# Startup loads on ScalarE's queue, spaced first scores and a re-planned attention stage: a decay-attention kernel with two dense layers

## The chip, the cores and the metric

The kernel runs on one core of one Trainium2 chip. The metric is the device time of one execution in microseconds; the number that counts is the median of several runs. One more execution is recorded by the hardware profiler, and all rows below come from it. The engines are PE (TensorE matmul; PEld is its weight load), DVE (VectorE), ACT (ScalarE), POOL (GpSimd) and SP (SyncE, which mostly issues DMAs).

## What is computed

Three layers follow each other on 4 batches of 8 heads, 576 tokens, head size 64 (2304 tokens of 512 features):

```
scores = q @ k.T / sqrt(64)
cum    = cumsum(log(clip(f, 1e-4, 1)), axis=-1)
scores = where(causal, -1e9, scores + cum[..., :, None] - cum[..., None, :])
attn   = exp(scores - max);  attn = attn / (sum(attn) + 1e-9)
x      = (attn @ v), heads side by side          # 2304 x 512
h = x @ w_in;  g = s * relu(h)**2 + b;  x = g @ w_out             # 512 -> 2048 -> 512
h = x @ w_in;  g = max(h, 0) + alpha * min(h, 0);  out = g @ w_out  # 512 -> 2048 -> 512
```

q, k, v, x and the outputs are fp32; the weights of the two dense layers come in 64-bit words and are split by the kernel into a high and a low part, so that each dense product is three matmul passes (high with high, low with high, high with low).

## The kernel before, in words

**One static order.** The program does not write its instructions in order of the source. It lists tasks (engine, planned cost, what they read and write, a priority), and `Scheduler.run` plays them through in a simulated time and issues on each engine, when that engine is free in the plan, the ready task with the lowest priority. What comes out is a fixed instruction order for each engine; on the chip the engines then wait for each other by semaphores. The priorities come from the table `PLAN`. A list of two options (`pick(PLAN["nr"], ...)`) lets the plan take whichever engine is free; a one-letter entry fixes the engine.

**Unread products.** While the plan's time is below `FILL` (50 us) and PE has nothing ready in the plan, `filler()` (L388) issues a 128x256 bf16 matmul of a tile of ones into a spare PSUM tile `h`. Nobody reads it. These products are in the static order too: each costs its time whether PE would have waited there or not.

**Startup.** SP's queue loads, in this order, the q and k rows of units 0 and 1 (`lk`, L314), the forget factors `ft`, the selector matrix `sel`, the first part of the causal mask, then weights (`raw`), identity and v. DVE clamps `ft` (L492), ACT takes the logarithm (L493, after a table load L478), DVE scans it into `ct` (L494), DVE and POOL make scaled and split copies (L497 to L506) that go out to DRAM and come back as extra rows of later `lk` tiles.

**Attention.** Work is cut into units: units 0 to 3 are two heads each with the 128-row chunks 0 and 1, then single heads of batch 0 with the chunks 2, 3 and 4, then whole heads of batches 1 to 3. For a chunk: scores on PE (L675 in fp32; L670 and L671 in high and low parts from the 13th unit on; unit 0 alone is L678, L679 and L681, where PE itself adds the decay from `ct` and `sel`), masked maximum on DVE (L689), exponential on ACT (L694), reciprocal of the sum on DVE (L697, L698), the norm, that is the division by the sum (L705, always POOL here, `nr="p"`), transposes on PE (L745), their copies out of PSUM on ACT (L754, L756), products with v on PE (L798), and the split of the result into high (L804) and low (L809). POOL also makes the high part of k and q (L610, L613), their difference (L619, `kl="p"`), and the low part of weights (L439); ACT and DVE convert the weights (L422; L413, L416, L419; L429).

**Dense part.** Between the attention tasks the plan puts the first half of the first dense layer for the blocks of 256 tokens 0 to 5 (L847 products into `h`, L884 into `a`). From about 334 us on only dense work is left: 512-wide products on L847, L882 and L887, with ACT and DVE making `r` and `g` between them. The last 128 rows of the output leave through two copies of one accumulator into one tile `o` and one DMA.

The lines that matter below:

```python
    startup(("sp", 200, lambda: load(ft, f)), w=["f"])
    hi="a", ev="a", xh="va", gh="va", kl="p", nr="p", lo="p",
    if eng == "pe" and free["pe"] <= now + 1e-6 and now < FILL and self.filler is not None and self.filler():
```

## Time and profile before

| | |
|---|---|
| median of 3 runs | 1007.63 us (1007.58, 1007.63, 1012.58) |
| the profiled execution's own time | 1007.88 us |
| its span, first to last instruction | 1006.1 us |
| outside the span | 1.78 us |
| PE busy | 997.2 us, 99% of the span |
| PE's share of the chain that ended last | 96% |

PE is the engine that sets the time. "Busy" on PE is not the same as useful: it includes the unread products. From 333.8 us to 1002.2 us PE is busy without a gap.

### The profile page before, as it was taken

The numbers are of one execution on the slowest core, as the hardware profiler recorded it, in microseconds if no ns is written. First come the engines' busy times: TensorE is split into PE (matmuls) and PEld (weight loads), VectorE is DVE, ScalarE is ACT, GpSimd is POOL, SyncE is SP. The second block draws the span as 40 slices with busy tenths as digits, with TensorE's granted clock in tenths as the row PEclk, the third lists the DMA queues.
The fourth block names the chain that finished last, engine by engine and source line by source line (L and its number), as shares of the span: only waits on it lengthen the run. The fifth ranks groups of instructions, "written<-read, shape, count | busy, mean of one in ns | idle before, by whom it ended". The sixth has DMA issues, their size and how long they took to land.

```text
span 1006.1 us, 15607 instructions
## 1 busy us (share of the span) xinstructions
PE 997.2 (99%) x5705; PEld 835.2 (83%) x5705; DVE 555.8 (55%) x1262; ACT 450.6 (45%) x1067; POOL 236.4 (24%) x275
## 2 busy tenths in 40 slices
PE   9999999999999999999999999999999999999998
PEld 7678889997989889888888888888888888888897
DVE  5888876576575688988342789323222322322232
ACT  5777766557566445555232445222222222222232
POOL 4656765465364144211000121000000000000000
PEclk9999999999999999999999999999999999999999
DMA  7765436234431544447352665003002100200010
GB/s 215 242 191 163 146 107 213 83 104 125 141 116 31 190 144 127 135 136 263 96 171 70 218 225 174 1 1 125 1 1 84 42 1 1 83 1 1 1 42 22
DMA packets 45519, 106.45 MB, mean 106 GB/s; under 512 B 4492, under 2 KB 23524, under 8 KB 44516
## 3 DMA queue, kind: packets, MB, share of 16 engines
q1 hardware_dynamic: 45444, 105.46, 32.7%
q8 instruction: 45, 0.74, 0.3%
q14 instruction: 30, 0.25, 0.1%
HBM read 77.65 MB, written 24.26 MB: 101 GB/s over the span
## 4 chain that ended last, share of the span: by engine, by line
PE 96%; ACT 1%; DMA 1%; DVE 1%; issue 1%; POOL 0%; ACTq 0%; POOLq 0%; SPq 0%
PE h L847 24%; PE k L847 16%; PE b L882 11%; PE a L884 9%; PE b L887 9%; PE a L882 9%; PE t L798 5%; PE t L745 4%; PE s L670 2%; PE a L887 2%; PE s L671 2%; PE h L388 2%; PE s L675 1%; DMA raw<-in_wi_dram 1%; ACT e L694 0%
## 5 line engine op out<-in xcount | busy, mean ns | idle before, releaser
L847 PE MATMUL h<-x,i 128*128 128x256 f32 (+1 forms) x1344 | 256.4, 340 | 0.3 <-DVE r L858 0.3
L847 PEld LDWEIGHTS h<-x,i 128*128 128x128 f32 x1344 | 210.9, 189 | 31.5 <-DVE r L858 0.9
L847 PE MATMUL k<-x,i 128*128 128x512 f32 (+1 forms) x672 | 153.4, 377 | 0.0
L847 PEld LDWEIGHTS k<-x,i 128*128 128x128 f32 x672 | 120.7, 188 | 25.5
L882 PE MATMUL b<-o,g 128*128 128x512 f32 x480 | 121.1, 393 | 0.0
L875 DVE TENSOR_TENSOR g<-r,g 128x512 fp32r<-128x512 f32 (+1 forms) x80 | 51.1, 639 | 121.0 <-ACT g L864 121.0
L705 POOL TENSOR_SCALAR e<-e,rec 128x128 f32<-128x128 f32 (+4 forms) x144 | 89.6, 634 | 90.5 <-DVE rec L698 40.8
L882 PEld LDWEIGHTS b<-o,g 128*128 128x128 f32 x480 | 90.2, 188 | 20.5
L439 POOL TENSOR_TENSOR i<-cv,i 128x512 fp32r<-128x512 f32 x32 | 49.7, 1554 | 243.9 <-ACT i L429 243.8
L864 ACT CAST g<-r 128x512 fp32r<-128x512 f32 (+1 forms) x78 | 45.1, 578 | 137.5 <-PE b L882 87.6
L884 PE MATMUL a<-g,o 128*128 128x256 f32 x768 | 104.5, 285 | 0.0
L882 PE MATMUL a<-o,g 128*128 128x512 f32 x384 | 98.8, 393 | 0.0
L884 PEld LDWEIGHTS a<-g,o 128*128 128x128 f32 x768 | 96.8, 190 | 1.2 <-issue 0.7
L887 PE MATMUL b<-g,o 128*128 128x512 f32 x384 | 95.3, 394 | 0.0
L873 DVE SCALAR_TENSOR_TENSOR g<-r,small,g 128x256 fp32r<-128x256 f32 (+1 forms) x104 | 70.6, 679 | 41.2 <-ACT g L866 40.1
L694 ACT ACTIVATE e<-e,ngm 128x128 f32<-128x128 f32 (+4 forms) x144 | 84.2, 586 | 15.4 <-DVE ngm L689 13.4
L887 PEld LDWEIGHTS b<-g,o 128*128 128x128 f32 x384 | 72.0, 188 | 16.8
L882 PEld LDWEIGHTS a<-o,g 128*128 128x128 f32 x384 | 71.1, 188 | 15.1
L866 ACT ACTIVATE g<-r,small 128x256 fp32r<-128x256 f32 (+1 forms) x90 | 53.3, 592 | 61.3 <-PE b L887 31.3
L689 DVE CUSTOM_DVE_ANT_0 e<-s,mask 128x128 f32<-128x128 f32 (+4 forms) x144 | 66.9, 480 | 18.3 <-PE s L671 7.3
L745 PE MATMUL t<-ident,e 128*128 128x128 f32 (+1 forms) x400 | 64.9, 275 | 3.5 <-ACT pt L754 2.1
L860 DVE SCALAR_TENSOR_TENSOR r<-k,sg_t,r 128x512 f32<-128x512 f32 (+1 forms) x40 | 27.9, 697 | 73.2 <-ACT r L854 73.2
(102 smaller groups left out, 1252.0 us busy)
## 6 DMA issues: line engine op xcount, KB each, us to landing
raw<-in_wi_dram SPq DMA_DIRECT2D x32, 512.0 KB
raw<-in_wo_dram SPq DMA_DIRECT2D x32, 512.0 KB
x<-x_d SPq DMA_DIRECT2D x7, 2048.0 KB
rawqk<-in_qk_dram SPq DMA_DIRECT2D x24, 576.0 KB
x_d<-o SPq DMA_DIRECT2D x36, 256.0 KB
v<-in_v_dram SPq DMA_DIRECT2D x20, 320.0 KB
x_d<-x SPq DMA_DIRECT2D x6, 1024.0 KB
out_dram<-o SPq DMA_DIRECT2D x18, 256.0 KB
```

Of the source, the lines that this page charges most:

```text
L689: nc.vector.tensor_tensor_reduce(e.t[0:rows, k0:k1], st_.t[0:rows, 0:w], mask[0:rows, m0:m0 + w], -0.125 if u.f32 else -1.0, init, ALU.add ...
L694: nc.scalar.activation(x, x, AF.Exp, bias=ng[0:rows, col:col + 1], scale=-1.0, accum_out=sm[0:rows, col:col + 1])
L705: eng.tensor_scalar(x, x, rc[0:rows, col:col + 1], 1.0, ALU.mult, ALU.mult)
L745: nc.tensor.transpose(pp.t[0:kw, i * P:i * P + P], e.t[:, P * kb:P * kb + kw], ident)
L798: nc.tensor.matmul(o.t[64 * j:64 * j + 64, a - q0:z - q0], vb.t[0:kr, kb, j, :], uu.pt[jj].t[0:kr, kb * PTS + a:kb * PTS + z], start=(i == ...
L847: nc.tensor.matmul(ps.t[:, 0:w], wv[:, wl, kc, :], x.t[:, kc, xl, x0:x0 + w], start=(n == 0), stop=(n == 3 * KC - 1))
L866: eng.activation(g.t[:, 0, 0:w], r.t[:, 0:w], AF.Identity, bias=b_t)
L873: nc.vector.scalar_tensor_tensor(g.t[:, 1, 0:w], r.t[:, 0:w], b_t, h, ALU.add, ALU.subtract)
L875: nc.vector.tensor_tensor(g.t[:, 1, 0:w], r.t[:, 0:w], h, ALU.subtract)
L882: nc.tensor.matmul(acc[u].t, g.t[:, gl, u * P:u * P + P], wo.t[:, wl, :], start=(first and i == 0), stop=end)
L884: nc.tensor.matmul(acc[u // 2].t[:, T * (u % 2):T * (u % 2) + T], wo.t[:, wl, u * P:u * P + P], g.t[:, gl, 0:w], start=(first and i == 0 a ...
L887: nc.tensor.matmul(acc[u].t[:, 0:w], wo.t[:, wl, u * P:u * P + P], g.t[:, gl, 0:w], start=(first and i == 0), stop=end)
```

## The change

Five things are changed at once.

1. `ft`, `sel` and the first part of the mask are issued by ScalarE's queue (a planner engine "aq"), ahead of ScalarE's first table load, and no longer by SP.
2. An unread product is put ahead of each of the three parts of unit 0's scores: 12 in all.
3. Loads are shorter: unit 0's `lk` comes in two halves of one head each; single-head units of batch 0 load their q and k only from the first row of q that they use.
4. The planner's cost for chunk 4 is changed, and the table `PLAN` is new. Norms may go to POOL, ACT or DVE (`nr="pav"`), the difference of k to POOL or DVE (`kl="pv"`), the high part of weights to DVE or ACT.
5. The last 128 output rows leave as two halves with a tile and a DMA of their own: columns 0 to 255 by DVE and SP's queue, 256 to 511 by ACT and ACT's queue.

```diff
-    hi="a", ev="a", xh="va", gh="va", kl="p", nr="p", lo="p",
+    hi="va", ev="a", xh="va", gh="av", kl="pv", nr="pav", lo="p",
...
-    startup(("sp", 200, lambda: load(ft, f)), w=["f"])
+    st.append(task(("aq", 200, lambda: nc.scalar.dma_start(ft, f)), w=["f"], prio=-300.0))
...
-    startup(("sp", 200, lambda: load(sel, sel_in)), w=["sel"])
+    st.append(task(("aq", 100, lambda: nc.scalar.dma_start(sel, sel_in)), w=["sel"], prio=-250.0))
...
+                q0 = P * u.chunks[0]
+                load(u.lk.t.bitcast(F32)[0:64].rearrange("d a s -> d (a s)")[:, q0:2 * S],
+                     qk[n, 0:64].rearrange("d a s -> d (a s)")[:, q0:2 * S])
...
+        if u.pe_rows:
+            for j in range(2):
+                h = slice(QA * j, QA * j + QA)
+                task(("sp", 0.9 * kb_of(P * 4 * w), lambda h=h: load(u.lk.t.bitcast(F32)[0:64, :, h], qka[n // 2][:, :, h])), w=[(U, "raw", j)],
+                     bufs=[u.lk], prio=-200.0 if j == 0 else pr)
...
                         n = uu.heads[j]
+                        sc.filler()
                         nc.tensor.matmul(x, lk[0:64, 0, q], lk[0:64, 1, k], start=True, stop=False)
+                        sc.filler()
                         nc.tensor.matmul(x, ct[:, 128 * c:128 * c + rows], sel[:, 0, n:n + 1].to_broadcast([NHEAD, nn]),
                                          start=False, stop=False)
+                        sc.filler()
                         nc.tensor.matmul(x, sel[:, 1, n:n + 1].to_broadcast([NHEAD, rows]), ct[:, k0:k1], start=False, stop=True)
...
-                for h, (e, cols) in enumerate((("act", slice(0, 288)), ("dve", slice(288, DM)))):
+                for h, (e, cols) in enumerate((("dve", slice(0, 256)), ("act", slice(256, DM)))):
+                    if h:
+                        o = R["o"].buf()
...
-                task(("sp", kb_of(P * 2048), lambda row=row, o=o: load(out[row:row + P, :], o.t)), r=[("ot", row, 0), ("ot", row, 1)], w=[("out", row)],
-                     bufs=[o], prio=epr)
+                    task((("sp", "act")[h], (kb_of(P * 1024), 600)[h],
+                          lambda f=(nc.sync.dma_start, nc.scalar.dma_start)[h], cols=cols, row=row, o=o: f(out[row:row + P, cols], o.t[:, cols])),
+                         r=[("ot", row, h)], w=[("out", row, h)], bufs=[o], prio=epr)
...
-        task(("sp", kb_of(P * 4 * (z - a)), lambda a=a, z=z: load(mask[:, a:z], mask_in[:, a:z])), w=[("mask", i)],
-             prio=PLAN["mp"] + PLAN["mq"] * (i > 0))
+        task(("sp" if i else "aq", kb_of(P * 4 * (z - a)), lambda i=i, a=a, z=z: (nc.sync if i else nc.scalar).dma_start(mask[:, a:z], mask_in[:, a:z])),
+             w=[("mask", i)], prio=PLAN["mp"] + PLAN["mq"] if i else -200.0)
```

**What the new order is at three places.** Line numbers of the changed kernel are higher by 8 to 27.

ScalarE at the start of the program, before:

```order
L478 ACT_TABLE_LOAD
L478 ACTIVATE small<-small 128x1
L493 ACTIVATE ft<-ft 32x256
L493 ACTIVATE ft<-ft 32x320
L503 ACT_TABLE_LOAD
```

and changed:

```order
L484 DMA ft<-in_f_dram 32x576
L487 DMA sel<-in_sel_dram 32x64
L1021 DMA mask<-in_mask_dram 128x256
L486 ACT_TABLE_LOAD
L486 ACTIVATE small<-small 128x1
L501 ACTIVATE ft<-ft 32x256
L501 ACTIVATE ft<-ft 32x320
```

Three DMA issues now stand ahead of the table load on ACT; on SP they are gone from behind the loads of `lk`.

PE around the first scores (`s`, unit 0), with `h` the tile of the unread products, before:

```order
L388 MATMUL h_114<-unit 128x256
L678 MATMUL s_192<-lk_112 128x128
L679 MATMUL s_192<-sel,ct 128x128
L681 MATMUL s_192<-ct,sel 128x128
L678 MATMUL s_202<-lk_112 128x256
L679 MATMUL s_202<-sel,ct 128x256
```

and changed:

```order
L396 MATMUL h_115<-unit 128x256
L699 MATMUL s_172<-lk_112 128x128
L396 LDWEIGHTS unit
L396 MATMUL h_115<-unit 128x256
L701 MATMUL s_172<-sel,ct 128x128
L396 LDWEIGHTS unit
L396 MATMUL h_115<-unit 128x256
L704 MATMUL s_172<-ct,sel 128x128
```

Unread products before: 43 ahead of the first scores, none among them, 29 behind them, 65 later, 137 in all. Changed: 27 ahead, 12 among them, 40 behind, 75 later, 154 in all. Every other matmul of PE is there in both, in the same number and shapes.

POOL where its first norms stand (`e` is a chunk's exponentials, `rec` the reciprocals of its sums), before:

```order
L439 TENSOR_TENSOR i_0_228<-cv_206,i_0_228 128x512
L439 TENSOR_TENSOR o_0_260<-cv_214,o_0_260 128x512
L705 TENSOR_SCALAR e_0_263<-e_0_263,rec_100 128x128
L705 TENSOR_SCALAR e_0_269<-e_0_269,rec_100 128x256
L705 TENSOR_SCALAR e_0_277<-e_0_277,rec_100 128x128
L705 TENSOR_SCALAR e_0_293<-e_0_293,rec_100 128x256
```

and changed:

```order
L447 TENSOR_TENSOR i_0_250<-cv_218,i_0_250 128x512
L728 TENSOR_SCALAR e_0_222<-e_0_222,rec_100 128x128
L447 TENSOR_TENSOR o_0_284<-cv_235,o_0_284 128x512
L447 TENSOR_TENSOR i_0_406<-cv_369,i_0_406 128x512
L728 TENSOR_SCALAR e_1_360<-e_1_360,rec_101 128x256
```

Of unit 0's four norms one is left on POOL. Over the whole program POOL had all 144 norms; now it has 66, ACT 48 and DVE 30. Of 24 differences of k 12 move from POOL to DVE; of the casts of x (L804) 20 move from ACT to DVE; of the high casts of weights (L429) 5 move from ACT to DVE.

SP at the end of the program, before:

```order
L314 DMA out_dram<-o_9316 128x512
L314 DMA out_dram<-o_9318 128x512
L314 DMA out_dram<-o_9676 128x512
L314 DMA out_dram<-o_9678 128x512
L1174 UNCONDITIONAL_BRANCH
```

and changed:

```order
L322 DMA out_dram<-o_9326 128x512
L322 DMA out_dram<-o_9328 128x512
L1002 DMA out_dram<-o_9688 128x256
L322 DMA out_dram<-o_9686 128x512
L1201 UNCONDITIONAL_BRANCH
```

The half tile of the last rows (`o_9688`) stands ahead of the whole tile of the 128 rows before them (`o_9686`, `o_9676` before the change); the other half is issued by ACT.

The order of the dense blocks among the attention tasks is new as well. Before, the longest stretch of PE's order with no dense matmul in it, from the attention's second half on, holds 34 transposes, 24 matmuls of scores and 28 of products. Changed, the longest holds 45 transposes, 42 matmuls of scores and 28 of products, and two more, with one group of dense matmuls between them, are about half and two thirds as long as the one before the change.

## Rows read from the trace of the kernel before

**Rows 1.** The page: engines' busy time and share, then the chain's shares.

```profile
PE 997.2 (99%) x5705; PEld 835.2 (83%) x5705; DVE 555.8 (55%) x1262; ACT 450.6 (45%) x1067; POOL 236.4 (24%) x275
...
PE 96%; ACT 1%; DMA 1%; DVE 1%; issue 1%; POOL 0%; ACTq 0%; POOLq 0%; SPq 0%
```

**Rows 2.** Stretch, length, busy us (count) of PE, PEld, DVE, ACT, POOL; clock, DMA share, GB/s.

```profile
25.00:75.00 50.00, 48.19 (x337) 34.37 (x335) 43.80 (x129) 39.42 (x112) 30.35 (x38) 1.00 0.73 215
25.00:334.00 309.00, 304.87 (x2389) 261.41 (x2388) 220.37 (x697) 205.57 (x631) 174.25 (x224) 1.00 0.46 142
333.80:1002.20 668.40, 668.40 (x3170) 555.63 (x3168) 320.10 (x513) 231.83 (x404) 50.87 (x32) 1.00 0.25 85
```

**Rows 3.** Timeline, 0 to 25 us: start, duration, engine, line, what, idle before.

```profile
0.73 1.28 ACT L478 ACT_TABLE_LOAD   x1 [0.73 <-PEq L1167]
...
0.74 1.32 SPq L314 DMA_DIRECT2D lk<-in_qka_dram  x2
...
0.89 6.91 PE L388 MATMUL h<-unit 128*128 128x256 bf16 x43 [0.89 <-POOL unit L347]
...
2.10 0.59 SPq L314 DMA_DIRECT2D ft<-in_f_dram  x1
...
6.10 0.52 DVE L492 TENSOR_SCALAR ft<-ft 32x256 f32<-32x256 f32 x2 [4.01 <-DMA ft<-in_f_dram]
6.42 0.78 ACT L493 ACTIVATE ft<-ft 32x256 f32<-32x256 f32 x2 [4.19 <-DVE ft L492]
6.87 0.68 DVE L494 TENSOR_TENSOR_SCAN ct<-c,ft 32x256 f32<-32x256 f32 x1 [0.25 <-ACT ft L493]
...
7.73 0.49 PE L678 MATMUL s<-lk 64*128 64x128 f32 x2
...
11.52 5.04 PE L388 MATMUL h<-unit 128*128 128x256 bf16 x29
...
16.49 0.70 PE L678 MATMUL s<-lk 64*128 64x256 f32 x2
...
22.82 1.62 PE L388 MATMUL h<-unit 128*128 128x256 bf16 x13
24.27 1.04 PE L675 MATMUL s<-lk 66*128 66x128 f32 x6
```

**Rows 4.** Unread products by stretch: length, busy PE, PEld; clock, DMA share, GB/s.

```profile
0.80:4.90 4.10, 4.01 (x19) 2.78 (x20) 1.00 0.65 152
5.00:7.70 2.70, 2.70 (x25) 2.23 (x23) 1.00 1.06 334
11.90:15.10 3.20, 3.20 (x17) 2.28 (x15) 0.50 0.65 139
```

**Rows 5.** Timeline of PE, 36 to 42 us, with one wait.

```profile
38.73 0.41 PE L745 MATMUL t<-ident,e 128*128 128x128 f32 x2 [1.31 <-ACT pt L754]
```

**Rows 6.** Waits of PEld, 25 to 334 us: total us, times, longest.

```profile
PEld t L745 <- POOL e L705: 2.9, 5, 1.9
```

**Rows 7.** Instruction groups by line and shape: count, busy us, mean ns.

```profile
L705 POOL TENSOR_SCALAR e<-e,rec 128x384 f32<-128x384 f32 x32 | 22.5, 702 | 22.0 <-ACT r L852 9.1 <-DVE rec L698 7.7 <-DVE ngm L689 3.1
L756 ACT COPY pt<-t 128x384 f32<-128x384 f32 x32 | 15.2, 475 | 3.9 <-PE t L745 3.5
```

**Rows 8.** The longest stretch without dense matmuls, columns as in Rows 2.

```profile
234.20:250.40 16.20, 15.06 (x117) 10.59 (x115) 11.43 (x43) 12.50 (x44) 11.52 (x17) 1.00 0.51 149
```

**Rows 9.** Timeline from 1000 us on: the end of the program.

```profile
1001.59 0.59 ACT L978 COPY o<-a 128x512 f32<-128x512 f32 x1 [1.70 <-PE a L882]
1002.20 1.27 SPq L314 DMA_DIRECT2D out_dram<-o  x2
1002.29 0.39 DVE L973 COPY o<-a 128x224 f32<-128x224 f32 x1 [1.94 <-PE a L882]
1002.71 0.40 ACT L973 COPY o<-a 128x288 f32<-128x288 f32 x1 [0.54 <-DVE o L973]
```

**Rows 10.** Busy time by stretch at the end; the last column is GB/s moved.

```profile
1003.00:1003.90 0.90, 0.00 (x0) 0.00 (x0) 0.00 (x0) 0.11 (x1) 0.00 (x0) 1.00 0.76 291
```

More of the change, by code (lines that the diff above doesn't have):

```diff
@@ L37 @@
 PLAN = dict(
-    t0=-3.05, ta=0.02, tb=9.58, t1=9.28, t2=12.15, t3=16.92,
-    prep=9.74, prepA=97.01,
+    t0=-8.65, ta=-2.52, tb=9.53, t1=10.2, t2=10.92, t3=20.92,
+    prep=7.78, prepA=71.98,
     nf=12,
-    cp=56.95, mp=-66.96, ip=-19.42, vp=-13.58, mq=75.16,
-    grp=2, grpA=3,
-    max=2.08, pv=10.38, f2=-11.55,
-    hi="a", ev="a", xh="va", gh="va", kl="p", nr="p", lo="p",
-    cv=(-57.21, -37.06, -8.25, 17.09, 19.42, 46.66, 50.1, 25.16, 9.28, 40.5, 51.51, 38.2, 27.17, 98.82, -3.43, 40.27),
-    blocks=((-15.09, 1.24), (1.24, 1.1), (1.1, 1.27), (1.28, 2.07), (2.07, 2.39), (3, 3)),
+    cp=113.38, mp=-56.63, ip=-41.35, vp=-5.36, mq=66.0,
+    grp=2, grpA=5,
+    max=1.6, pv=-3.8, f2=-6.04,
+    hi="va", ev="a", xh="va", gh="av", kl="pv", nr="pav", lo="p",
+    cv=(-50.71, -64.33, -17.63, 24.13, -0.63, -29.95, 22.81, -46.43, -28.66, 20.48, 29.71, 48.44, -5.27, 109.41, 17.13, 52.3),
+    blocks=((-31.69, 2.46), (2.27, 3), (3.3, 2.67), (2.67, 2.52), (2.64, 3.13), (3, 2.54)),
     )
@@ L121, in task @@
         return t
-    LAT = {"pe": 0.0, "dve": 140.0, "act": 200.0, "pool": 150.0, "sp": 0.0, "py": 0.0}
-    FAR = {"pe": 220.0, "dve": 90.0, "act": 90.0, "pool": 60.0, "sp": 30.0, "py": 0.0}
+    LAT = {"pe": 0.0, "dve": 140.0, "act": 200.0, "pool": 150.0, "sp": 0.0, "aq": 0.0, "py": 0.0}
+    FAR = {"pe": 220.0, "dve": 90.0, "act": 90.0, "pool": 60.0, "sp": 30.0, "aq": 30.0, "py": 0.0}
     def run(self):
-        engines = ("py", "sp", "pe", "act", "dve", "pool")
+        engines = ("py", "sp", "aq", "pe", "act", "dve", "pool")
         free = dict.fromkeys(engines, 0.0)
@@ L185, in start @@
                     arm(x, now)
-            if e == "sp":
+            if e == "aq":
+                self.wire = max(self.wire, now + 1000.0) + ns
+                free[e] = now + 600.0
+                free["act"] = max(free["act"], now) + 600.0
+                push(self.wire + 700.0, "end", t, e)
+                push(free[e], "idle", None, e)
+                push(free["act"], "idle", None, "act")
+            elif e == "sp":
                 self.wire = max(self.wire, now + 1000.0) + ns
@@ L572, in t_load @@
         def t_load():
-            load(u.lk.t.bitcast(F32)[0:64, :, 0:w], qka[n // 2] if u.two else qk[n, 0:64])
+            if u.two:
+                load(u.lk.t.bitcast(F32)[0:64, :, 0:w], qka[n // 2])
+            else:
+                q0 = P * u.chunks[0]
+                load(u.lk.t.bitcast(F32)[0:64].rearrange("d a s -> d (a s)")[:, q0:2 * S],
+                     qk[n, 0:64].rearrange("d a s -> d (a s)")[:, q0:2 * S])
         def t_rows():
@@ L581, in t_rows @@
                 load(dst, c8_d[n].rearrange("a r s -> r a s"))
-        task(("sp", 1.8 * kb_of(P * 4 * w), t_load), w=[(U, "raw")], bufs=[u.lk], prio=pr)
-        if not u.pe_rows:
+        if u.pe_rows:
[3 more added lines that the diff above has]
+                     bufs=[u.lk], prio=-200.0 if j == 0 else pr)
+        else:
+            task(("sp", 1.8 * kb_of(P * 4 * w if u.two else 256 * (2 * w - P * u.chunks[0])), t_load), w=[(U, "raw")], bufs=[u.lk], prio=pr)
             task(("sp", 700 if u.two else 100, t_rows), r=[("c8d", 0)] + ([] if u.two else [("c8d", 1)]), w=[(U, "rows")], bufs=[u.lk], prio=pr)
@@ L708, in scores @@
             for uu in us:
-                cyc += 4 * max(CW[c], 760 * (c == 4)) * (3.6 if uu.pe_rows else 1) if uu.f32 else [288, 288, 422, 556, 640][c] * 2
+                cyc += (2 if c == 4 and u.f32 and u.mate.f32 else 4) * max(CW[c], 720 * (c == 4)) * (3.6 if uu.pe_rows else 1) if uu.f32 else [288, 288, 422, 556, 640][c] * 2
                 if uu.pe_rows:
-                    need += [(uu.i, "raw"), "sel", ("c", 0), ("c", 1)]
+                    need += [(uu.i, "raw", j), "sel", ("c", 0), ("c", 1)]
                 else:
@@ L971, in finish_out @@
             if row == NT - P:
[L972 to L973 removed]
+                for h, (e, cols) in enumerate((("dve", slice(0, 256)), ("act", slice(256, DM)))):
+                    if h:
+                        o = R["o"].buf()
+                    task((e, 400, lambda f=(nc.vector.tensor_copy, nc.scalar.copy)[h], cols=cols, o=o, u=u: f(o.t[:, cols], acc[u].t[:, cols])),
                          r=[AK], w=[("ot", row, h)], bufs=[acc[u], o], prio=epr)
[L975 to L976 removed]
+                    task((("sp", "act")[h], (kb_of(P * 1024), 600)[h],
+                          lambda f=(nc.sync.dma_start, nc.scalar.dma_start)[h], cols=cols, row=row, o=o: f(out[row:row + P, cols], o.t[:, cols])),
+                         r=[("ot", row, h)], w=[("out", row, h)], bufs=[o], prio=epr)
                 continue
```

1 line of the change is left out of this document (removed).

## The prediction, made before the changed kernel was run

> **What bounds the kernel now.** I read the page's first and fourth part first: PE is busy for 997.2 of 1006.1 us and makes up 96% of the chain that ended last [rows 1]. So an engine's time matters only where PE waits for it, and the next view is busy time by stretch. In the dense part PE is busy for all of 668.40 us [rows 2]. Its matmuls are the same after the change, so nothing is won or lost there. From 25 to 334 us PE is busy for 304.87 of 309.00 us [rows 2], so 4.13 us of visible waiting is all that a better order can take away there. The third view is the timeline of the first 25 us. There PE is "busy" with unread products: 43 from 0.89 to 7.73 us, when the first scores start, and 29 from 11.52 to 16.49 us [rows 3]. These 11.8 us and the 65 later ones are the largest piece that can be recovered, but only as far as the new order holds fewer or quicker ones, since each costs its time even where nobody waits.
>
> **Price of an unread product.** Three rows give it. In the first 4.1 us 19 take 4.01 us, 0.211 each; from 5.0 us on 25 take 2.70, 0.108 each; from 11.9 on 17 take 3.20, 0.188 each, and only there does the clock column show 0.50, the lower of the two levels (1.2 of 2.4 GHz) [rows 4]. In the first stretch the column says 1.00, but the pace is that of the lower level; I go by the pace. A later run of 13 lasts from 22.82 to 24.27 us, 0.111 each [rows 3]. I take 0.11 for one at the full clock.
>
> **Edit 1 and the shorter first load: when the first scores can start.** Before, SP issues both `lk` loads first (1.32 us) and `ft` at 2.10 us; DVE gets it at 6.10, the scan ends at 6.87 + 0.68 = 7.55 us, PE starts at 7.73 [rows 3]. Now ACT issues `ft` at about 0.73 us, where its first instruction stood, beside a `lk` load of half the size. 128 KB of `lk` and 72 KB of `ft` at the 152 GB/s of that stretch [rows 4] take 1.3 us. With some 1.4 us from issue to first bytes `ft` is there at about 3.4 us. That 1.4 is an estimate: it leaves 4.0 us from issue to landing before, less 584 KB at 223 GB/s, a rate between the 152 and the 334 of rows 4. The logarithm also needs ACT's table, and three issues now stand ahead of that: 0.73 + 3 x 0.5 (SP's issue of `ft` took 0.59) + 1.28 + 0.2 = 3.7 us. Then as before 0.45 us to the scan and 0.86 from there to PE [rows 3], so the scores could start at 5.0 to 5.3 us. PE's 27 products end at 0.89 + 19 x 0.211 + 8 x 0.108 = 5.8 us. So PE sets the start, with 0.5 us of cover. A table load that comes 0.5 us later costs nothing, beyond that all of it.
>
> A rule speaks against this edit. The Trainium skill, page "DMA: Bandwidth & Descriptors", section "Issuing engines are not separate DMA queues", says that DMAs from several engines run on the same 16 DMA engines, and that only the issuing sequencer's time is saved. By it `ft` would gain just its place in the queue, 2.10 − 0.73 = 1.37 us, the scores could start at 6.4, PE would wait 0.6 us behind its products, and the sum below would be 0.6 us higher. No row here shows two issuing engines at once; a result on the same side of every bound, so no rival.
>
> **Edit 2 and the counts of unread products.** Before: 6.84 us for the 43 (0.89 to 7.73), 4.97 for the 29, 65 x 0.11 = 7.15, together 18.96. Now: 4.9 for the 27; for the 12 among the first scores between 0 (they fill gaps between dependent small matmuls) and 12 x 0.11 = 1.3, I take the middle, 0.65, since the three score parts took 11.52 − 7.73 = 3.79 us [rows 3] with short gaps that I can't see whole; for the 40 behind them 4.4 at the full clock; 75 x 0.11 = 8.25. Together 18.2, **−0.8 us**, between −1.4 and −0.1. The real scores and products around them are the same. What must be ready at the end of the 40 (about 16 us) is the next scores' rows, which went out to DRAM and back; they start from `ct`, which is over 2 us earlier, so I cost that at nothing.
>
> **The wait at 38.7 us.** PE's transposes wait 1.31 us there [rows 5]; the profile names ACT's copy, and behind it PEld waits 1.9 us for a norm on POOL, the longest of its kind [rows 6]. POOL does the norms one by one behind slow weight work; a 384-wide norm costs it 0.702 us, where a copy of that width costs ACT 0.475 [rows 7]. With most of unit 0's norms off POOL, and half of all, I take this wait as gone: **−1.3 us** (bounds −1.3 and 0: another engine can be late there).
>
> **The middle, 39 to 334 us.** Of PEld's 2.9 us for norms on POOL 1.0 is left [rows 6] and should go: −1.0. Against it stands load. ACT gets 48 norms at 0.475 us and loses 25 casts at its mean of 205.57/631 = 0.33 us: +14.6, from 67% to 71% of the 309 us. DVE gets 67 instructions at its mean of 0.32, with the k differences longer: +21 to +30, from 71% to about 80%; from 25 to 75 us it is at 43.80 of 50 already [rows 2]. POOL goes from 56% to about a third. On average all this is hidden under PE; it isn't where PE has no dense work. The longest such stretch before takes 16.2 us, with PE idle for 1.14 and ACT busy for 12.50 [rows 8]. The new order has one of 115 matmuls in place of 86, 1.34 times, and two more of about 1.1 times together. At the same idle share that is 1.14 x 0.34 + 1.14 x 1.1 = 1.6; I take +1.4, since stretches like the two exist before too. **+0.4 us** for the middle, bounds −2.8 (all of the 4.13 less the 1.31) and +8.6 (third rival).
>
> **Shorter loads of the single heads, the planner's chunk-4 cost** cost or give nothing of their own: the waits of PE that I count are on copies and norms [rows 5, 6], and the order they make is in the terms above.
>
> **Edit 5, the end.** Before, the first of the two last DMAs is issued at 1002.20, and both (524 KB) move from about 1003.0 to 1004.8 at 291 GB/s [rows 9, 10]. ACT's last copy waits 0.54 us for DVE's [rows 9]. Now the half tile's DMA stands ahead of the whole tile on SP, and it waits for DVE's copy of 256 columns, 2.29 + 0.39 x 256/224 = 1002.74 us. So the whole tile, ready since 1002.18, goes out over half a microsecond later, and nothing moves before 1003.5. At 334 GB/s [rows 4] 524 KB end at 1005.1 in place of 1004.8: **+0.3 us**, between +0.5 (291 GB/s) and −0.3 (the rate holds and the half on ACT's queue goes first).
>
> **Sum.** −0.8 − 1.3 + 0.4 + 0.3 = −1.4 us on the profiled execution: 1007.88 − 1.4 = 1006.5. That execution is 0.25 us above the median of the runs, so 1006.2 is the forecast. 0.5% of this kernel is 5.0 us, about what a measurement can tell from no change: below 1002.6 is faster, above 1012.7 slower.
>
> **Rivals.**
>
> *All of PE's visible waits go.* Norms on three engines never let a transpose wait, and the 12 products hide whole: −4.13 (all waits of 25 to 334 us), −1.4, −0.3 at the end: −5.8, **1001.8 us**. For it: the waits named are on norms and copies. Against it: ACT's copies, the larger part, get more company, not less. Matmuls that follow each other late but with no visible gap could give a little more, to about 1000.
>
> *The longer attention-only stretches run at DVE's pace (slower).* In the stretch of rows 8 DVE's work goes with the scores: 11.43 x 42/24 = 20.0 us, and some 4 norms at its mean of 0.32 make it 21.3; ACT's goes with the transposes: 12.50 x 45/34 = 16.5, and 6 norms make it 19.4; PE has 15.06 x 1.34 = 20.1. Before, the stretch lasted 1.30 times as long as its busiest helper was busy (16.2/12.50); 1.30 x 21.3 = 27.7 us in place of 21.6 by PE's pace is +6.1, and with half as much for the two others (2.5) +8.6. With −0.8, −1.3, −1.0 and +0.3 that is +5.8, **1013.4 us**. It decides the sign once these three stretches lose 7.9 us or more. Against it: the planner knows these loads and fills POOL instead, which is at 11.52 of 16.2 there.
>
> *The clock falls again behind the first scores.* 17 of the 40 products at 0.188 and not 0.11 is +1.3: **1007.5**. For it: it did just that at 11.8 us before [rows 4]; against it: PE was on short, spaced scores ahead of that, and now has products between them.
>
> *ScalarE's queue brings `ft` no earlier.* The scores stay at 7.73 and PE waits 1.9 us: **1008.1**.
>
> **How the numbers follow.** The forecast has 0.56, the clock 0.06, the late `ft` 0.04, together 0.66 within 0.5%; the first rival 0.20, the second 0.14. The range runs from 1000.0, which takes in most of the first rival, to 1013.5, the middle of the second; some 0.05 lie below and 0.1 above.
>
> **What would show it.** First scores at 5.8 us; 40 unread products in 4.4 us at clock 1.00; the next scores at 16 to 17; no wait above 0.5 us on the transposes before 52 us; the dense part 668.4 us long, beginning 1 to 2 us earlier than 333.8; last bytes 0.3 us later, counted from PE's end. I am wrong if the dense part begins above 5 us off in either direction: then the middle decides, by waits of the transposes on a norm or a copy.

## The result, and the profile after

The changed kernel is slower, by a little over 1%. In three runs it took 1019.92 to 1023.64 us, where the kernel before took 1007.58 to 1012.58: a ratio of 1.0127, 95% interval 1.0102 to 1.0153. A fourth run, the one that was profiled, ran in a slower state at a mean granted clock of 0.789 (1170.85 us) and is left out of the comparison. Measured again beside the experiments (r1 below) it was 1.0107, interval 1.0086 to 1.0129, median 1019.22 us. The forecast was 1006.2 with a range of 1000.0 to 1013.5.

The trace read here is therefore that of r1's profiled execution: 1019.1 us, span 1017.3 us, against 1007.88 and 1006.1 before. First the page's busy times, then busy time by stretch (columns as in rows 2): behind the first scores, the attention part, the dense part.

```profile
PE 1006.1 (99%) x5722; PEld 838.3 (82%) x5722; DVE 570.7 (56%) x1323; ACT 467.6 (46%) x1088; POOL 166.2 (16%) x185
```

```profile
11.40:21.50 10.10, 10.10 (x36) 5.83 (x36) 4.50 (x13) 3.06 (x8) 3.02 (x3) 0.50 0.64 195
25.00:344.00 319.00, 312.89 (x2435) 267.10 (x2435) 236.77 (x765) 230.10 (x670) 113.43 (x139) 1.00 0.45 138
344.60:1013.00 668.40, 668.40 (x3171) 555.65 (x3168) 321.85 (x522) 227.41 (x395) 46.22 (x32) 1.00 0.25 85
```

The dense part is 668.4 us long as in [rows 2], but begins at 344.6 and not at 333.8. PE is busy 99% of the span in both: on such a kernel the share of busy time doesn't show 11 us of loss. PE's visible idle time between 25 us and the dense part grew only from 309.00 − 304.87 = 4.13 us [rows 2] to 319.00 − 312.89 = 6.11 us. Three marks of PE's timeline split the 11.2 us between the spans. The first is the first dense matmul, before and changed:

```profile
43.95 1.68 PE L847 MATMUL h<-x,i 128*128 128x256 f32 x12
```

```profile
49.88 1.69 PE L870 MATMUL h<-x,i 128*128 128x256 f32 x12
```

| | before | changed | difference | forecast |
|---|---|---|---|---|
| first dense matmul starts ("start") | 43.95 | 49.88 | +5.93 | −2.1 |
| from there to the end of attention ("middle") | 289.81 | 294.71 | +4.90 | +0.4 |
| dense part | 668.49 | 668.48 | 0 | 0 |
| from PE's last matmul to the end of the span | 3.85 | 4.25 | +0.40 | +0.3 |

The start in PE's timeline, with the columns of rows 3:

```profile
0.89 4.90 PE L396 MATMUL h<-unit 128*128 128x256 bf16 x27 [0.89 <-POOL unit L355]
5.72 0.48 PE L699 MATMUL s<-lk 64*128 64x128 f32 x2
6.14 0.28 PE L396 MATMUL h<-unit 128*128 128x256 bf16 x1
6.35 0.48 PE L701 MATMUL s<-sel,ct 32*128 32x128 f32 x2
...
12.12 0.39 PE L396 MATMUL h<-unit 128*128 128x256 bf16 x1
12.44 1.22 PE L699 MATMUL s<-lk 64*128 64x256 f32 x2
...
16.54 7.03 PE L396 MATMUL h<-unit 128*128 128x256 bf16 x40
23.41 0.49 PE L768 MATMUL t<-ident,e 128*128 128x128 f32 x3
```

The other engines at the same place, from the whole timeline:

```profile
0.74 0.39 ACTq L484 DMA_DIRECT2D ft<-in_f_dram  x1
...
2.67 0.52 DVE L500 TENSOR_SCALAR ft<-ft 32x256 f32<-32x256 f32 x2 [0.58 <-DMA ft<-in_f_dram]
...
18.23 0.67 DVE L728 TENSOR_SCALAR e<-e,rec 128x256 f32<-128x256 f32 x2
18.30 0.51 ACT L726 ACTIVATE e<-e,rec 128x256 f32<-128x256 f32 x1
18.30 0.53 POOL L728 TENSOR_SCALAR e<-e,rec 128x128 f32<-128x128 f32 x1 [2.24 <-DVE rec L721]
```

`ft` is there at 2.7 us and the first scores start at 5.72, behind their 27 products: the early start that edit 1 was to bring is there. But a product between two scores costs 6.35 − 6.14 = 0.21 us, and 0.32 from 12.1 us on. The granted clock is at its lower level from 11.34 to 21.58 us, 10.24 us against 3.41 before. From the first scores to the 40 products PE takes 16.54 − 5.72 = 10.82 us; the same scores took 3.79 us and, for the last of the four groups, 18.18 − 16.49 = 1.69 us before, 5.48 in all. Their end in the kernel before:

```profile
18.18 0.92 PE L675 MATMUL s<-lk 66*128 66x128 f32 x4
```

And all four norms of unit 0 are done at 18.9 us, while PE works through its 40 products until 23.41: the norms need none of the last 4.5 us of them.

One trace shows one execution, and the clock differs between executions of one order. Three kernels below (r9, r10, r13) have the order of the kernel before on PE for the first 75 us. In the four traces the lower level lasts 3.41 us (before), 3.41 (r13), 10.24 in two pieces (r10) and not at all (r9), and the first dense matmul starts at 43.95, 44.25, 46.83 and 43.75 us. The mean clock of each run helps to tell an edit from this spread: all seven compared runs of the changed kernel stand at 0.991 to 0.996, while the runs of the kernel before reach from 0.993 to 1.000.

### The profile page after: what moved, and what is told of

Same layout as the page of the kernel before. It is cut to its first block, busy times and chain, and to the rows that moved or that the text cites. A ratio compares the mean times of both kernels' runs of the same rounds, so it can differ in the third digit from the quotient of the medians.

```text
span 1169.1 us, 15492 instructions
## 1 busy us (share of the span) xinstructions
PE 1160.9 (99%) x5722; PEld 909.7 (78%) x5722; DVE 563.8 (48%) x1323; ACT 470.9 (40%) x1088; POOL 163.2 (14%) x185
## 3 DMA queue, kind: packets, MB, share of 16 engines
q1 hardware_dynamic: 45348, 104.60, 27.7%
## 4 chain that ended last, share of the span: by engine, by line
PE 99%; ACT 0%; DVE 0%; issue 0%; POOL 0%; POOLq 0%
PE h L870 24%; PE k L870 16%; PE b L905 10%; PE a L907 9%; PE b L910 9%; PE a L905 8%; PE t L821 5%; PE t L768 5%; PE a L910 2%; PE s L690 2%; PE s L695 2%; PE h L396 2%; PE s L691 2%; PE s L704 0%; PE s L699 0%; PE s L701 0%
## 5 line engine op out<-in xcount | busy, mean ns | idle before, releaser
L870 PE MATMUL h<-x,i 128*128 128x256 f32 (+1 forms) x1344 | 293.6, 374 | 0.7 <-DVE r L881 0.6
L870 PEld LDWEIGHTS h<-x,i 128*128 128x128 f32 x1344 | 229.5, 203 | 49.9 <-issue 1.6
L870 PE MATMUL k<-x,i 128*128 128x512 f32 (+1 forms) x672 | 171.9, 410 | 0.0
L907 PE MATMUL a<-g,o 128*128 128x256 f32 x768 | 122.5, 318 | 0.0
L907 PEld LDWEIGHTS a<-g,o 128*128 128x128 f32 x768 | 114.4, 213 | 3.1 <-issue 1.6
L910 PE MATMUL b<-g,o 128*128 128x512 f32 x384 | 113.9, 450 | 0.0
L896 DVE SCALAR_TENSOR_TENSOR g<-r,small,g 128x256 fp32r<-128x256 f32 (+1 forms) x104 | 64.7, 623 | 63.5 <-ACT g L889 63.0
L717 ACT ACTIVATE e<-e,ngm 128x256 f32<-128x256 f32 (+4 forms) x144 | 84.0, 585 | 15.8 <-DVE ngm L712 15.3
L881 DVE SCALAR_TENSOR_TENSOR r<-h,small,r 128x256 f32<-128x256 f32 (+1 forms) x76 | 43.1, 568 | 89.7 <-ACT r L875 89.6
L712 DVE CUSTOM_DVE_ANT_0 e<-s,mask 128x256 f32<-128x256 f32 (+4 forms) x144 | 67.3, 481 | 35.8 <-PE s L695 12.4
L875 ACT ACTIVATE r<-h 128x256 f32<-128x256 f32 (+1 forms) x76 | 34.3, 451 | 94.7 <-PE h L870 94.7
```

Of the source, the lines that this page charges most:

```text
L712: nc.vector.tensor_tensor_reduce(e.t[0:rows, k0:k1], st_.t[0:rows, 0:w], mask[0:rows, m0:m0 + w], -0.125 if u.f32 else -1.0, init, ALU.add ...
L717: nc.scalar.activation(x, x, AF.Exp, bias=ng[0:rows, col:col + 1], scale=-1.0, accum_out=sm[0:rows, col:col + 1])
L870: nc.tensor.matmul(ps.t[:, 0:w], wv[:, wl, kc, :], x.t[:, kc, xl, x0:x0 + w], start=(n == 0), stop=(n == 3 * KC - 1))
L896: nc.vector.scalar_tensor_tensor(g.t[:, 1, 0:w], r.t[:, 0:w], b_t, h, ALU.add, ALU.subtract)
L907: nc.tensor.matmul(acc[u // 2].t[:, T * (u % 2):T * (u % 2) + T], wo.t[:, wl, u * P:u * P + P], g.t[:, gl, 0:w], start=(first and i == 0 a ...
L910: nc.tensor.matmul(acc[u].t[:, 0:w], wo.t[:, wl, u * P:u * P + P], g.t[:, gl, 0:w], start=(first and i == 0), stop=end)
```

## The experiments

Times are medians beside the kernel before on the same chip; a ratio is to that, with its 95% interval. Two edits are used that keep every other instruction in place: an unread product that the plan counts but that isn't issued, and an instruction issued to another engine at its place in the program. "Lost" time in a stretch is start to start of PE's matmuls, less the lower quartile of the same shape in the kernel before; the length of a stretch "at the lower quartile" is the sum of these quartiles.

### r1: the changed kernel again

> The changed kernel, unaltered, for a trace of an execution at the full clock. Theory M (the new table's order makes PE wait in the attention part): the dense part, 668.4 us long, begins 8 to 12 us later than the 333.8 us of before, and the lost time stands as waits of transposes and products between 39 and 340 us. Theory C (the clock falls for longer in the first 50 us, since the mean clock of the changed kernel is 0.991 to 0.995 against 0.998): the stretch at the lower level lasts 7 us or more longer than the 3.4 us of before and accounts for over half of the 12 us; waits from 39 us on add under 3 us. Both: time near 1022 us, ratio 1.010 to 1.015.

1019.22 us, ratio 1.0107. Neither theory alone: start and middle are both late, as in the table above. The dense part begins 10.8 us later, as M had it; the lower level lasts 6.8 us longer, just short of C's 7.

### r2 and r7: the products around the first scores, taken out and put in

```diff
-                        sc.filler()
                         nc.tensor.matmul(x, lk[0:64, 0, q], lk[0:64, 1, k], start=True, stop=False)
-                        sc.filler()
...
-                        sc.filler()
```

(r2 takes these three lines out of the changed kernel, r7 puts them into the kernel before.)

> The changed kernel without the 12 unread products around the first scores; every other instruction keeps its place on every engine. M: 0 to 1.3 us faster than the changed kernel, no more. C, if the spaced products are what lets the clock fall: 3 us or more faster than the changed kernel; if they hold the clock up: 2 us or more slower.

> The kernel before with the 12 unread products around its first scores and no other edit; all else keeps its place. Theory H (each of them costs its own time and the restart of the next score, 0.21 us at the full and 0.33 us at the lower level, and the lower level lasts longer): 2.5 to 6 us slower than before. Rival (they hide in gaps between the scores): 0 to 1.3 us slower.

Without them 1016.19 us, ratio 1.0053 (1.0030 to 1.0077): 3.0 us less by the medians, 5.4 by the ratios, which is C's side. The first dense matmul starts 3.3 us earlier, at 46.56. Put into the kernel before they cost 1013.57 against 1009.02, ratio 1.0046 (1.0030 to 1.0062), and the first dense matmul starts 4.4 us later. r7's timeline:

```profile
8.22 0.28 PE L388 MATMUL h<-unit 128*128 128x256 bf16 x1
8.44 0.48 PE L681 MATMUL s<-sel,ct 32*128 32x128 f32 x2
...
15.37 5.03 PE L388 MATMUL h<-unit 128*128 128x256 bf16 x30
20.32 0.70 PE L679 MATMUL s<-lk 64*128 64x256 f32 x2
```

Nothing hides: 0.22 us each at the full clock. The lower level lasts 6.83 us here against 3.41, a difference within the spread of executions. One product between two scores did not hold the clock up, in either kernel. Both runs agree within the intervals, so this edit alone is some 3 to 5 us of the loss.

### r6: three products in place of one

```diff
-                        sc.filler()
+                        for _ in range(3):
+                            sc.filler()
...
```

(The same at all three places.)

> The changed kernel with three unread products where it has one around the first scores (36 in place of 12); nothing else moves. Theory S (short scores with one product between them leave PE too thinly occupied, and the clock falls behind them): the stretch at the lower level shrinks from 10.2 us to 3.5 or less, which gives back 3 us, against 24 x 0.11 = 2.6 us of added products: 1017 to 1020 us. Rival N (what lies between the scores doesn't matter to the clock): about 10 us at the lower level again, 2.6 us or more slower than the changed kernel.

1020.89 us, ratio 1.0118 (1.0099 to 1.0138): no different in time. But the clock stays up behind the first scores. The same stretch as in r1, and the 40 products behind it:

```profile
11.40:21.40 10.00, 10.00 (x70) 6.80 (x69) 5.36 (x16) 3.90 (x10) 3.02 (x3) 1.00 0.57 164
155.00:179.00 24.00, 22.02 (x137) 14.74 (x135) 16.70 (x64) 18.06 (x56) 9.07 (x14) 0.86 0.51 159
```

```profile
16.99 4.66 PE L396 MATMUL h<-unit 128*128 128x256 bf16 x40
21.49 0.49 PE L771 MATMUL t<-ident,e 128*128 128x128 f32 x3
```

The 40 products take 4.5 us and not 6.87, as the forecast had it, and the first transposes come 1.92 us earlier than in r1 with 24 more products issued. So the trace is on theory S's side for the clock: with PE fuller between the scores it doesn't fall. One trace alone wouldn't show it, since r9's doesn't fall either without any such product; but the four runs of r6 have mean clocks of 0.996 to 1.000, against 0.991 to 0.996 in the seven of the changed kernel. The 1.92 us are gone by 75 us (the same matmuls stand 0.1 us later than in r1), and this execution lost 3.4 us more at a fall from 171.75 to 178.57 us (second row), at the end of the longest stretch of attention matmuls.

### r12: fewer products behind the first scores

```diff
+        count[0] += 1
+        if 26 < count[0] <= 50:
+            return True
         nc.tensor.matmul(fill_tile[0][:, 0:256], unit[:, 0:1].to_broadcast([P, P]), unit[:, 1:2].to_broadcast([P, 256]), start=True, stop=True)
...
```

(The three lines of r2 are taken out as well.)

> The changed kernel without the 12 unread products around the first scores, and with 16 in place of 40 behind them; all else keeps its place. Theory T (the norms of unit 0 are done at 16.2 us there, and PE runs unread products until 19.7: too many are counted): the first transposes at 16.5 to 17.2, 2 to 3.5 us faster than without the trim, near 1013. Rival (the lead is lost to a later load or wait, as after the earlier start of the kernel before): within 1 us of the untrimmed one, 1016.

1011.58 us, ratio 1.0026 (1.0013 to 1.0039), against r2's 1.0053: 2.7 us less by the ratios, 4.6 by the medians. The two intervals overlap, so by the times alone r12 isn't clearly faster than r2; against the changed kernel itself (1.0086 to 1.0129) it is. r12's timeline:

```profile
13.75 3.59 PE L399 MATMUL h<-unit 128*128 128x256 bf16 x16
17.14 0.84 PE L768 MATMUL t<-ident,e 128*128 128x128 f32 x3
```

The transposes start at 17.14 without a wait, 2.6 us earlier than in r2, and the lead is still 2 us or more at the end of attention. r2 and r12 together take away three quarters of the changed kernel's excess (1.0107 to 1.0026). In r12's trace the first dense matmul starts at 44.57 us, 0.62 later than before in place of 5.93, and the middle is as long as in r1 (4.95 us more than before): in these traces these products were nearly the whole of the start's share, and none of the middle's.

### r14: are the later products needed at all?

```diff
+        if count[0] > 72:
+            return True
```

> The kernel before without the 65 unread products behind 16.5 us; the 72 ahead stay. Theory T (a fixed count of unread products is paid whether PE would wait or not): PE waits where they stood, but for less than their 7.3 us, and the dense part begins 1 to 4 us earlier, unless the lead is lost to the weight loads near 60 us. Rival C (they keep the clock up): a stretch at 0.50 of 3 us or more between 17 and 60 us that before doesn't have, and the time 1 us or more slower.

1019.59 against 1008.10 us, ratio 1.0105 (1.0087 to 1.0123): the rival. Without its 65 later products the kernel before runs at the lower level from 19.92 to 57.47 us:

```profile
20.00:57.00 37.00, 33.52 (x113) 20.21 (x114) 19.97 (x75) 19.78 (x62) 15.68 (x25) 0.50 0.61 184
```

All five runs have a mean clock of 0.981 or 0.982. So an unread product has two sides. Behind the point where PE's next real work is ready it costs its time (r12). Elsewhere it can hold the clock: leaving 7 us of them out between 18.9 and 40.6 us cost 11.5 us (r14).

### r8 and r11: the earlier start, in the kernel before

```diff
+    nc.scalar.dma_start(ft, f)
+    nc.scalar.dma_start(sel, sel_in)
+    nc.scalar.dma_start(mask[:, 256:512], mask_in[:, 256:512])
-    startup(("sp", 200, lambda: load(ft, f)), w=["f"])
+    startup(("sp", 200, lambda: None), w=["f"])
...
+    fill_tile, skip = [], [16]
```

> The kernel before in its own order, with the forget factors, the selector and the first mask part issued by ACT's queue ahead of everything, unit 0's q and k in two halves, and 16 of the 43 unread products ahead of the first scores left out. If the earlier start is kept: first scores at 5.7 to 6.6 us, the dense part 1 to 2 us earlier, 1 to 2.5 us faster than before. Rival (a later wait or the clock takes it back): the dense part within 0.5 us of before, or a longer stretch at the lower level, and the time within 1 us or slower.

1008.95 against 1009.02 us, ratio 0.9995 (0.9980 to 1.0010). The first scores start at 5.63 us, 2.1 us earlier, and up to 64 us every matmul keeps about that lead (2.0 us at 55 us). At 64 to 66 us of before's time 1.7 us of it vanish. Timeline of r8 there:

```profile
60.37 0.68 ACT L425 ACTIVATE raw<-raw 128x512 f32<-128x512 f32 x1 [1.99 <-DMA raw<-in_wo_dram]
...
63.64 2.42 PE L809 MATMUL t<-pt,v 128*64 128x320 f32 x18 [0.43 <-ACT pt L767]
```

ACT takes its instructions in order. Its conversion of a weight waits 1.99 us for the load and holds the exponentials and copies behind it. Before, ACT reaches that conversion at 60.38 us, as late as here:

```profile
60.38 0.69 ACT L422 ACTIVATE raw<-raw 128x512 f32<-128x512 f32 x1
```

The load was issued 2.0 us earlier (54.87 against 56.85) and still came in only at 60.3, while before it was there when ACT came to it. Why it took 5.4 us here, and at most 3.5 before, isn't settled; the next weight load follows 1.4 us behind it in both. Two more small waits take the rest. In this execution that is where the faster start went: into ACT's wait for a load at 60 us. The median of r8 holds something else too: five of its twelve runs have a mean clock of 0.993 or 0.994 and took 1009.30 to 1011.83 us, the seven at 0.998 or 1.000 took 1006.68 to 1009.05.

r11 adds the shorter loads of single heads and the split end, with SP sending the whole tile ahead of the half one.

> The kernel before in its own order with three of the edits, in the form that the runs favour: the loads on ACT's queue with 16 unread products left out ahead of the first scores, the shorter q and k loads of single heads, and the last rows as two halves with the whole tile ahead of them on SP. If the 2 us won at the start were lost at 64 us to a weight load that came late, and 64 KB less per head bring it earlier: 1 to 2.5 us faster than before; the lead after 66 us is 1 us or more (0.3 without the shorter loads). If not: within 0.5 us of before. End: 0.2 to 0.4 us shorter than before from PE's last matmul.

1008.65 against 1009.40 us, ratio 0.9984 (0.9970 to 0.9998), the only version that beats both kernels, by little, and less than was expected if the lead were kept. It isn't kept beyond 66 us in its trace either: 1.4 us of it went at 38 to 42 us, where that execution's clock fell for 3.41 us, the rest at 64 to 66. So the shorter loads did not remove the wait: ACT waits 1.33 us for the same load until 61.40 us, though it was issued at 56.58, 0.3 us earlier than before. That load took 4.8 us, so it came late by itself and not only because ACT was early. The end is 3.56 us from PE's last matmul, 0.29 less than before.

### r9 and r10: longer stretches of attention matmuls, norms on POOL

```diff
-    blocks=((-15.09, 1.24), (1.24, 1.1), (1.1, 1.27), (1.28, 2.07), (2.07, 2.39), (3, 3)),
+    blocks=((-15.09, 1.24), (0.89, 1.1), (1.1, 1.27), (1.28, 2.07), (2.07, 2.39), (3, 3)),
```

(r9. r10 has (1.28, 0.82) in place of (1.28, 2.07) and nothing else.)

> The kernel before with one number of its table changed (the second block's start, 1.24 to 0.89). The first 120 us of PE's order are word for word those of before, norms stay on POOL; but the attention matmuls between two groups of dense ones now come in two long stretches (10.9 and 8.2 us at their lowest price) in place of one (8.2). Theory O (attention matmuls without dense ones between them lose about as much again in waits, whoever does the norms, and that is the changed kernel's middle): the dense part begins 3.5 to 7 us later, 4 to 8 us slower than before, and the loss stands in the new stretch. Rival L (the loss comes from norms on ACT and DVE, the order doesn't matter): within 1.5 us of before.

> The kernel before with another number changed (the fourth block's end, 2.07 to 0.82): one stretch of 22.9 us in place of 8.2, the rest of the order before it unchanged, norms on POOL. O: 7 to 13 us slower than before, the loss in that stretch; if the clock also falls in such stretches, a record of 0.50 lies inside it or at its end, 3 to 10 us long. L: within 1.5 us of before.

r9: 1012.06 us, ratio 1.0024 (1.0011 to 1.0037), 2.7 us slower: between theory and rival. Its middle is 2.5 us longer: 8.9 us are lost in the new stretch, but 6.5 fewer in the short ones that it is made of. r10: 1025.23 us, ratio 1.0153 (1.0135 to 1.0171), 15.8 us slower and so beyond O's 13; the middle is 15.5 us longer. Its stretch from 216 to 267 us, and the end of that:

```profile
216.00:267.00 51.00, 41.39 (x281) 29.57 (x280) 33.23 (x120) 31.96 (x108) 34.89 (x47) 0.93 0.39 113
256.50:263.00 6.50, 6.21 (x25) 4.76 (x27) 2.92 (x15) 5.17 (x17) 4.72 (x10) 0.50 0.43 116
```

PE idles 9.6 us there, and the clock falls to 0.50 inside it. So the order alone costs time: in r10 more than in proportion to the stretch (29.0 us lost in one of 21.1 at the lower quartile, where the longest of before loses 8.5 in 7.6), in r9 less (8.9 in 10.1). The changed kernel's two longest stretches together hold about as much as r9's two (16.8 and 17.6 us at the lower quartile; the two longest of before hold 11.2), which makes 2.5 us of its 4.9 an estimate for the order. Another estimate goes by all stretches. In those of 2.5 us or more at the lower quartile, the kernel before loses 26.1 us in 29.3 and the changed one 37.8 in 42.4, 0.89 per us in both; in the shorter ones 27.9 in 63.5 and 21.0 in 50.6. By before's two rates the new lengths alone would lose about 6 us more. So the order may be the whole of the middle; this is worked out, not tested.

### r5 and r13: who does the norms, in a fixed order

```diff
-                              a=("act", act(CW[c_], False, 1), lambda f=f_: f(nc.scalar))), r=[(PK_, "r")], w=[(K_, "e")], bufs=[e_], prio=pr_)
+                              a=("act", act(CW[c_], False, 1), lambda f=f_: f(nc.gpsimd))), r=[(PK_, "r")], w=[(K_, "e")], bufs=[e_], prio=pr_)
```

(r5, in the changed kernel. r13 issues the norms of the kernel before in turn to POOL, ACT and DVE.)

> The changed kernel in its own order on every engine, but ACT's 48 norms are issued to POOL at the same places of the program. Theory L (ACT's added load makes its copies out of PSUM late): PE's and PEld's waits on those copies fall from 7.7 us to 4 or less, waits on POOL's norms rise from 1.2 by 1 to 2 us, and the time falls by 2 to 4 us. Rival O (the order on PE, with its longer attention-only stretches, is what waits, whoever does the norms): waits on copies stay above 6 us and the time within 1 us of the changed kernel.

> The kernel before in its own order on PE, with its 144 norms issued in turn to POOL (66), ACT (48) and DVE (30), the shares of the changed kernel; nothing else moves. Theory L (norms on ACT and DVE put load in front of the copies and casts that PE waits for, and that is the half of the changed kernel's middle that its longer stretches don't explain): the dense part begins 2 us or more later, waits on ACT's copies rise from 2.1 us to 5 or more, 1.5 to 5 us slower than before. Rival P (it is POOL that is late in a given order, and relieving it helps): waits on POOL's norms fall from 2.7 us to 1 or less, 0 to 3 us faster.

r5: 1023.42 us, ratio 1.0145 (1.0131 to 1.0160), slower still than the changed kernel. PEld's waits on copies fell from 7.7 to 3.8 us, as theory L had it, but waits on POOL's norms rose from 1.2 to 4.6 and others came; the sum was worse. r13: 1012.54 against 1008.10 us, ratio 1.0042 (1.0028 to 1.0055). PEld's waits in r13, and in r1 as the changed kernel:

```profile
PEld h L851 <- DVE r L862: 2.0, 3, 1.1
PEld t L802 <- ACT pt L760: 1.9, 4, 0.5
PEld t L749 <- POOL e L709: 1.7, 2, 1.3
```

```profile
PEld t L768 <- ACT pt L779: 4.9, 10, 1.4
...
PEld t L821 <- ACT pt L779: 1.8, 4, 0.9
...
PEld t L768 <- ACT pt L777: 1.2, 3, 0.4
...
PEld t L768 <- POOL e L728: 1.0, 1, 1.0
```

From 30 us on, PEld's waits on ACT's copies are 2.1 us before, 4.5 in r13 and 7.7 changed; on POOL's norms 2.7, 1.7 and 1.2. PE's own waits on POOL's norms rose in r13 from 0 to 0.9 us, so that relieving POOL helped isn't shown; loading ACT and DVE cost more: r13's middle is 3.6 us longer than before, in an order that is the same on PE. That is the price of norms spread in turn over an order that was planned for POOL. In the order that was planned for three engines, taking the norms back to POOL (r5) is worse than leaving them. So neither run gives the norms' share of the changed kernel's middle.

### r3 and r4: the table in the other kernel

```diff
-    t0=-8.65, ta=-2.52, tb=9.53, t1=10.2, t2=10.92, t3=20.92,
+    t0=-3.05, ta=0.02, tb=9.58, t1=9.28, t2=12.15, t3=16.92,
...
```

> The changed kernel with the table of the kernel before (norms on POOL, old priorities); startup queue, products between the scores, shorter loads and the split end stay. M: the loss is gone, 1004 to 1009 us. C (startup edits lower the clock): 1015 us or more.

> The kernel before with the new table alone (norms on three engines, new priorities); startup on SP, no products between the scores, full loads, one tile at the end. M: 1015 us or more, the dense part beginning 8 us or more later. C: within 3 us of the kernel before.

1027.23 us, ratio 1.0179 (1.0163 to 1.0195), and 1034.19, 1.0248 (1.0221 to 1.0274): both worse than either kernel. By the letter r3 met C and r4 met M. The table and the rest don't add: each new combination makes another order, whose three longest stretches together hold 21 us in r3 and 29 in r4 at the lower quartile, with falls of the clock at 94 to 98 and 108 to 115 us in r3 and 132 to 142 us in r4. They say that a table is worth what its own order is worth, and nothing about which of the two parts of the change is to blame.

## Why the prediction was wrong, step by step

- **First scores.** 5.72 us, forecast 5.8. `ft` was there at 2.7 us, not 3.4. By the rule that I weighed (the Trainium skill, page "DMA: Bandwidth & Descriptors", section "Issuing engines are not separate DMA queues") they would have started at 6.4. The trace shows nothing against the rule; what I derived from it was wrong. I took over the 4.0 us from issue to landing of before, and these hold the 512 KB of `lk` that SP had issued ahead of `ft` there [rows 3]. In r1 `ft` is issued together with the first `lk` and is there 1.9 us later. In r4, where the new table lets SP issue `ft` ahead of `lk`, it is there as early:

```profile
0.74 0.39 SPq L314 DMA_DIRECT2D ft<-in_f_dram  x1
...
2.70 0.52 DVE L492 TENSOR_SCALAR ft<-ft 32x256 f32<-32x256 f32 x2 [0.61 <-DMA ft<-in_f_dram]
```

So it was the place ahead of `lk` that brought `ft` early, and no run shows that ACT's queue added to it.
- **The price of the products among the scores: the step that failed first.** Forecast 0 to 1.3 us, taken 0.65. Measured: the scores with their products took 10.82 us where the scores took 5.48, 5.3 us more. Of that, 2.7 are 11 products at 0.21 or 0.32 us (one of the 12 is the last of the 27 ahead, so 26 and 76 stand where I counted 27 and 75). Some 0.5 are scores that take 0.42 us in place of 0.32 behind a product, and 2.2 are the last four, which ran at the lower level. I bounded a product by its own time in a long row of its kind, 0.11 [rows 3, 4], but that is a price in a row of products; between two small scores it took about twice as much.
- **The 40 behind them.** Forecast 4.4 us at the full clock, measured 6.87. The rival "the clock falls again" named the mechanism, with 17 products and +1.3 us and a chance of 0.06. The lower level lasted 10.24 us and slowed the last scores too. The argument against it, that products between scores would hold the clock, was wrong for one product; with three the clock held in r6's trace.
- **What the count is measured against.** The forecast compared the numbers of products before and after. It should have compared their end with the moment when the next real work is ready: 23.4 against 18.9 us. The forecast took the next scores for the work behind the 40, ready at about 16 us, and costed it at nothing; what stands there is unit 0's transposes, which need its norms. Without 24 of them the first transposes start 2.6 us earlier than in r2, without a wait (r12). The 76 later ones took 9.4 us in place of 8.25.
- **The wait at 38.7 us** is gone: the trace shows no wait of PE between 17 and 52 us. So the term of −1.3 came true, within a start that lost far more. That the norms did it isn't shown: in r9, with the order and the norms of before, PE's waits on copies between 30 and 52 us are 0.6 us in place of 1.3.
- **The middle: the second step that failed.** Forecast +0.4, measured +4.9. The forecast priced the new, longer stretches by PE's visible idle share in one of them, 1.14 of 16.20 us [rows 8], and took +1.4. Visible idle time is the wrong price: start to start, that same stretch loses 8.5 us against the lower quartile, since its matmuls follow each other late while PE still counts as busy. The rival of the longer stretches had the right place, at the wrong engine and a wrong price. It forecast 27.7 us for the longest stretch, at DVE's pace; the stretch took 22.0, with ACT busier than DVE:

```profile
154.10:176.10 22.00, 20.02 (x145) 14.26 (x144) 17.05 (x66) 18.73 (x59) 9.08 (x14) 1.00 0.53 164
```

The waits that grew most are on ACT's copies. How the 4.9 us divide between the order and the norms stays open: r9 gives about 2.5 for the order and the rates of all stretches some 6, while r13 gives 3.6 for norms in an order not made for them. The forecast priced an ACT norm by a copy out of PSUM, 0.475 us [rows 7]. The norm itself took 0.616. What was left on POOL took 0.835 in place of 0.702 at 384 columns; at 512 columns nothing rose (0.743 and 0.750), and in r13, with the same shares, POOL's 384-wide norms took 0.592.

```profile
L728 POOL TENSOR_SCALAR e<-e,rec 128x384 f32<-128x384 f32 x11 | 9.2, 835 | 14.2 <-DVE rec L721 9.6 <-PE s L691 2.9 <-ACT pt L779 1.2
...
L726 ACT ACTIVATE e<-e,rec 128x384 f32<-128x384 f32 x12 | 7.4, 616 | 3.8 <-DVE rec L721 3.8
```

- **The end.** +0.40 us, forecast +0.3. SP sends the half tile first, and the whole tile, copied by 1012.99, only at 1013.98:

```profile
1012.40 0.59 ACT L1005 COPY o<-a 128x512 f32<-128x512 f32 x1 [1.70 <-PE a L905]
1013.11 0.42 DVE L999 COPY o<-a 128x256 f32<-128x256 f32 x1 [1.95 <-PE a L905]
1013.56 0.33 SPq L1002 DMA_DIRECT2D out_dram<-o  x1
...
1013.98 0.38 SPq L322 DMA_DIRECT2D out_dram<-o  x1
```

Turned around in r11 the same split is 0.29 us shorter than before.

- **The sum.** Start +5.9, middle +4.9, end +0.4 are the 11.2 us between the two spans. The range missed because the slower cases of start and middle were weighed one at a time, and the start's at 1.3 us; here both came.

## What to carry to other kernels

Filler work in a fixed order is to be judged at two points: whether the engine's clock falls without it, and whether the next real work is ready before the filler ends; its own price per piece comes last, and is to be read where the piece will stand. A gain at the start is not yet a gain of the whole: look for the next load with little cover before adding it to a sum. Moving work off a waiting engine is priced at the engine that receives it, in the stretches where the main engine has nothing else to do, and not by mean loads or by the main engine's visible idle time.

## What the runs showed of the hardware

- The granted clock fell to 0.50 where PE was busy in its record: in r1 at 11.34 us, during small scores with one product between them, and PE is busy for all of 11.40 to 21.50 us. In some executions it fell late in the longest attention stretches as well (r6 at 171.75, r10 at 256.4 us; not in r1 and r12, which have r6's stretch). Without the later fillers it stayed there for 37.5 us, though PE was busy for 33.52 of 37 (r14).
- The same first 75 us of PE's order gave no fall in r9, 3.41 us in the kernel before and in r13, and 10.24 in r10.
- Runs of one kernel spread with the clock: of 29 runs of the kernel before (those beside r9 to r12), the 19 at a mean clock of 0.997 to 1.000 took 1007.55 to 1010.45 us, and the 10 at 0.994 to 0.996 took 1010.49 to 1012.73.
- A transfer of 72 KB that was issued first was there 1.9 us after its issue on ACT's queue (r1) and 2.0 us on SP's (r4); on SP's queue behind 512 KB it took 4.0 us (before).
